# Second product of the last tile as seven block products, three of them after the last quartet

## The chip, the cores and the metric

The kernel runs on one core of a Trainium2 chip. The metric is the device time of one execution in microseconds (us). Each result is the median of several runs; the profile is of one execution.

## The reference

Nystrom attention for 4 batches, 8 heads, 576 positions and head dimension 64 feeds two feed-forward blocks of 2304 tokens, model width 512 and inner width 2048. All inputs are fp32. The change is in the second block:

```python
h = x @ w_in                                                  # 2304x512 @ 512x2048
g = np.where(h > 0.0, h, alpha * (np.exp(np.minimum(h, 0.0)) - 1.0))
return (g @ w_out).astype(np.float32)                         # 2304x2048 @ 2048x512
```

## The kernel before

Attention and block 1 come first and end some 430 us after the start; block 2 fills the rest. It works in NTT = 3 tiles of 768 tokens, each of two halves of T2 = 384 tokens, and each tile in NQ = 8 quartets. A quartet makes 256 of the 2048 inner columns: r and r + 8 of 16 column blocks of 128, for both halves, so four blocks (i, c) of 128x384.

A product of two fp32 matrices is made of three matmuls: each operand is split into a high part (a cast) and a low part (the value less the cast), and high x high, high x low and low x high are added up. `to_pair` (ScalarE for the cast, VectorE or GpSimd for the low part) does the splitting.

**First product** (`quartet`). It already is a product of seven blocks in Winograd's form of Strassen's method: seven products of 2x2 blocks instead of eight, with sums before and after. The sums of x lie on chip for a tile (`x_places`, `load_x`), those of w_in come from DRAM (`load_in2`). Each of seven steps p runs one block product, six matmuls of 384 columns, into one of two PSUM banks "h". VectorE adds the running sums to it, and `elu` makes a block of g: an add on VectorE out of PSUM, two activations on ScalarE, a combine on VectorE, then the pair. The pairs lie in a ring of eight places.

**Second product** (`second`, before the change everywhere). Per quartet: six groups of 128 tokens x two column blocks x three terms = 36 matmuls with a 128x128 piece of g as the loaded weight and 512 columns of w_out as the moving operand. They add up over the eight quartets in six PSUM banks (tags "bk" and "x"), are copied out in the last quartet (`ob`) and stored. The pairs of w_out come from DRAM (`wo2p`, written in the first tile) into a ring of NS = 4 places, two per quartet (`load_out2`).

**Order.** All matmuls of block 2 go through `bmm`, which chains each to the one before: PE's order is that of the program text. The loop at the end of the kernel runs `quartet` step by step and after each step some five or six matmuls of the second product, which lags by one quartet and one step (`behind`). What is left after the last quartet is run by `run(behind)`: 42 matmuls of 512 columns. On the other engines a planner orders the instructions by a priority (`wanted`) and its own estimate of times, and each engine then runs them strictly in that order. All DMAs are issued from SP in order; a DMA that waits for its place holds up those behind it.

`load_x(t + 1, pool)` prepares the sums of x of the next tile on GpSimd during the current one, so GpSimd works in the first two tiles of block 2 and is idle in the third. `scratch` takes its room from a ring of three. The places of an odd tile's x are free while an even tile is worked on, and in the last tile no next tile fills them.

The profile names nearly every instruction by one line, L110, the helper that records it. Tiles therefore tell what is what: h and x are PSUM banks (x also the sums of x), w the pairs of w_out, wi those of w_in, gf/gh/gl/ghl the blocks of g and their parts, y the sum inside `elu`, a and u the running sums, ob the output rows. PE is TensorE, DVE VectorE, ACT ScalarE, POOL GpSimd, SP the engine that issues the DMAs.

Of the kernel before, what the change touches and what calls it, by code (L numbers as in the profile page):

```python
# [10 lines left out]
F32 = mybir.dt.float32  # L11
F32R = mybir.dt.float32r
# [3 lines left out]
ALU = mybir.AluOpType  # L16
# [15 lines left out]
def nystrom_ffn_kernel(ctx: ExitStack, tc, q, k, v, w_in1, w_out1, w_in2, w_out2, out):  # L32
# [32 lines left out]
    B, G, _, _, S = q.shape  # L65
    D = 64
    H = 4 * G
    NDM, DM = w_in1.shape[2], w_in1.shape[2] * 128
# [3 lines left out]
    HALF = S // 2  # L72
# [6 lines left out]
    T2 = 384  # L79
    NS2 = T2 // 128  # L80
# [8 lines left out]
    NQ = NKT // 2  # L89
    NTT = NT // (2 * T2)  # L90
    LAG = 1
    T1 = 320
    YB, UB, SE = 2, 3, 1
    PRE, NLEAD, EI, EO = 2, 2, 3, 4
# [41 lines left out]
    ft = ctx.enter_context(tc.tile_pool(name="ft", bufs=2, reuse_waits="tile"))  # L136
    att = ExitStack()
# [13 lines left out]
    def wanted(s):  # L151
        tc.cur_priority = int(1000 * (s + 100))
# [33 lines left out]
    wo2d = dram.tile([NKT, 128, DM], F32, name="wo2d")  # L186
    wi2d = dram.tile([NQ, 2, 128, W], F32, name="wi2d")
    wi2p = dram.tile([NQ, 2, 2, 128, 7 * 128], F32, name="wi2p")
    wo2p = dram.tile([NKT, 2, 128, DM], F32, name="wo2p")

    banks, marks = {}, {}

# [108 lines left out]
    def to_pair(f, h, l, eng=vec):  # L301
        act.copy(out=h, in_=f)
        sub(l, f, h.bitcast(F32), eng)
# [4 lines left out]
    wo, wo2, wi, free = {}, {}, {}, {}  # L308
# [55 lines left out]
    PLACES = [f"wo{(kk - 2) % (NKT + 1)}" for kk in range(NKT + 1)]  # L364
    NS = 4

    late_out = []

    def load_out2(q):

        for i in range(2):
            kk = q % NQ + i * NQ
            t = wop.tile([128, 2, DM], F32, name="w2", tag=PLACES[(2 * q + i) % NS])
            hl = t.bitcast(F32R)
            if q < NQ:
                l = t[:, 1, :]
                sp.dma_start(out=l, in_=wo2d[kk])
                to_pair(l, hl[:, 0, :], hl[:, 1, :], pool)
                late_out.append((wo2p[kk].rearrange("x p n -> p x n"), t))
            else:  # L380
                sp.dma_start(out=t, in_=wo2p[kk].rearrange("x p n -> p x n"))
            wo2[q, i] = hl[:, 0, :], hl[:, 1, :]
# [407 lines left out]
    def span(b, hf):  # L790

        n = T1 if b == 0 else HALF
        return (0, n) if hf == 0 else (n, S - n)
# [57 lines left out]
    gt, acc = {}, {}  # L851
# [113 lines left out]
    def bmm(*a):  # L965

        inst = mm(*a)
        if chain[0] is not None:
            after(inst, chain[0])
        chain[0] = inst.ins  # L970

    def elu(key, src, add):

        n = made[0] % 8
        made[0] += 1
        if n < GB:
            h = gp.tile([128, T2], F32R, name="gh", tag="gh")
            l = gp.tile([128, T2], F32R, name="gl", tag="gl")
        else:
            t = nat.tile([128, G, W], F32R, name="ghl", tag=("nh2", "nl2", "nh3")[n - GB])  # L980
            h, l = t[:, 0, 0:T2], t[:, 1, 0:T2]
        gf = ft.tile([128, T2], F32, name="gf", tag="gf", bufs=2)
        c = stg.tile([128, W], F32, name="y", tag="y", bufs=YB)[:, 0:T2]
        vec.tensor_tensor(out=c, in0=src, in1=add, op=ALU.add)
        act.activation(out=gf, in_=c, func=AF.Relu, scale=-1.0)
        act.activation(out=gf, in_=gf, func=AF.Exp, scale=-1.0)
        vec.scalar_tensor_tensor(out=gf, in0=gf, scalar=-1.0, in1=c, op0=ALU.add, op1=ALU.max)
        to_pair(gf, h, l)
        gt[key] = h, l

    made = [0]

    def quartet(q):
# [24 lines left out]
        elu((q, 0, 0), block(1, 1), a1)  # L1018
        yield
        add(u3, block(3, 5), u2)  # L1020
        yield
        ps = block(4, 3)
        elu((q, 1, 1), ps, u3)
        add(u2, ps, u2)
        yield
        elu((q, 1, 0), block(2, 6), u3)
        yield
        elu((q, 0, 1), block(6, 2), u2)
        yield

    def second(q):

        for s in range(2 * NS2):
            if q % NQ == 0:
                acc[s] = (banks["x"] if s > 1 else banks["att"]).tile(
                    [128, 512], F32, name="x", tag="x" if s > 1 else "bk"
                )[:, 0:DM]
            sl = slice(s % NS2 * 128, s % NS2 * 128 + 128)
            for i in range(2):
                gh, gl = gt[q, i, s // NS2]  # L1040
                wh, wl = wo2[q, i]
                for j, (x, w) in enumerate(((gh, wh), (gh, wl), (gl, wh))):
                    bmm(acc[s], x[:, sl], w, q % NQ == 0 and i == j == 0, q % NQ == NQ - 1 and i == 1 and j == 2)
                    yield
            if q % NQ == NQ - 1:
                ob = nat.tile([128, G, HALF], F32R, name="ob", tag=("ath0", "ath1", "atl0")[s % 3])
                ob = ob.bitcast(F32).rearrange("p g t -> p (g t)")[:, 0:DM]
                (vec.tensor_copy if s % 2 else act.copy)(out=ob, in_=acc[s])
                r0 = q // NQ * 2 * T2 + s * 128
                sp.dma_start(out=out[r0:r0 + 128, :], in_=ob)  # L1050

    NA = B * SB

# [138 lines left out]
    for i in range(END, NA):  # L1192
        b, r = i // SB, i % SB
# [39 lines left out]

    def seconds():
        for q in range(NTT * NQ):
            yield from second(q)

    flush()
    wanted(NA - 6)
# [1 line left out]
    behind, tail, xs, n = seconds(), late(), x0, 0  # L1241
    for q in range(NTT * NQ):
        wanted(NA + 4 * q - 2)
        if q:
            load_in2(q + 1) if q + 1 < NTT * NQ else None
        if q % NQ == XPACE and q // NQ + 1 < NTT:
            xs = load_x(q // NQ + 1, pool)
        steps_ = quartet(q)
        for p in range(7):
            if p == 2:  # L1250
                load_out2(q)
            wanted(NA + 4 * q + 4 * p / 7 + 4)
            if conv and p % 2 == 0:
                conv.pop(0)()
            next(xs, None)
            wanted(NA + 4 * q + 4 * p / 7)
            next(steps_)
            for _ in range(2):
                next(tail, None)
            while n < (7 * q + p + 1 - 7 - LAG) * 12 * NS2 // 7:  # L1260
                next(behind)
                n += 1
        run(steps_)
# [37 lines left out]
```

## Time and profile before

| what | value |
|---|---|
| median of 3 runs | 825.69 us (821.93 to 826.5) |
| span of the profiled execution (the page gives no other time of it) | 824.7 us |
| PE busy | 788.3 us, 96% of the span |
| DVE, ACT, POOL busy | 62%, 54%, 41% |
| chain that ended last: PE, DVE, DMA, ACT | 75%, 12%, 5%, 3% |
| matmuls of 384 columns (first product of block 2) | 1008, 205.7 us |
| matmuls of 512 columns (second product of block 2) | 864 in three groups |
[...]

Busy times of matmuls overlap: one counts until its modelled end, while the next has started. How long a matmul takes of PE's time is read from the starts of two that follow each other.

### The profile page before, as it was taken

The page shows a single profiled execution, that of the slowest core. Times are in us where ns is not written, and L with a number is a line of the kernel's source. Part 1 is how long each engine was busy: PE and PEld are TensorE (multiplying, and loading weights), DVE is VectorE, ACT ScalarE, POOL GpSimd, SP SyncE. Part 2 cuts the span into 40 slices and gives each one's busy share as a digit, 9 for nine tenths or more (in the row PEclk, how much of TensorE's full clock was granted, in tenths as well). Part 3 has the DMA queues.
Part 4 walks back from the last instruction along what each step waited for, and adds up shares of the span by engine and source line. Part 5 has one row for each costly group of instructions (what it writes and reads, how often), then busy time and mean ns, then how long its engine had stood idle before and what let it go on. Part 6 is the DMA issues. An engine that isn't in the chain of part 4 may idle for free.

```text
span 824.7 us, 15400 instructions
## 1 busy us (share of the span) xinstructions
PE 788.3 (96%) x5644; PEld 689.3 (84%) x5644; DVE 508.2 (62%) x1026; ACT 446.1 (54%) x977; POOL 335.8 (41%) x348
## 2 busy tenths in 40 slices
PE   6699999999999999999997999999999999999998
PEld 3476777688997889889997999988989999999996
DVE  6898677457645754486347677656665455545543
ACT  3687554656656656574555556646454334434433
POOL 2566566557654665456438654620560000000000
PEclk9799999999999999999999999999999999999999
DMA  9966932685667445662442476777744655753632
GB/s 331 404 174 226 318 109 85 189 275 186 210 215 261 157 140 177 223 192 100 154 161 89 166 282 235 272 255 267 275 157 156 223 182 180 257 201 141 211 121 77
DMA packets 95563, 165.63 MB, mean 201 GB/s; under 512 B 7232, under 2 KB 51264, under 8 KB 95488
## 3 DMA queue, kind: packets, MB, share of 16 engines
q1 hardware_dynamic: 95488, 164.66, 58.6%
q8 instruction: 44, 0.72, 0.4%
q14 instruction: 31, 0.25, 0.1%
HBM read 119.54 MB, written 45.09 MB: 200 GB/s over the span
## 4 chain that ended last, share of the span: by engine, by line
PE 75%; DVE 12%; DMA 5%; ACT 3%; issue 2%; POOL 2%; SPq 0%; DVEq 0%; ACTq 0%; POOLq 0%
PE x L110 40%; PE h L110 29%; PE bk L110 6%; DVE u L110 1%; DVE h L110 1%; DMA u<-in_moe_w_in 1%; DVE y L110 1%; DVE nl L110 1%; DVE w1c L110 1%; POOL x L110 1%; DVE gf L110 1%; DVE lm L110 1%; DMA qt<-in_q 1%; DMA kt<-in_k 1%; DVE st L110 1%
## 5 line engine op out<-in xcount | busy, mean ns | idle before, releaser
L110 PE MATMUL h<-x,wi 128*128 128x384 f32 x1008 | 205.7, 339 | 1.1 <-DVE u L110 0.6
L110 PE MATMUL x<-gh,wo 128*128 128x288 f32 (+1 forms) x896 | 198.6, 297 | 0.8 <-ACT xs L110 0.4
L110 PEld LDWEIGHTS h<-x,wi 128*128 128x128 f32 x1008 | 182.1, 189 | 14.9 <-DVE u L110 1.0
L110 PEld LDWEIGHTS x<-gh,wo 128*128 128x128 f32 x896 | 149.1, 188 | 11.0 <-issue 7.2
L110 PE MATMUL x<-gl,wo 128*128 128x288 f32 (+1 forms) x448 | 130.6, 294 | 0.0
L110 ACT CAST gh<-gf 128x288 fp32r<-128x288 f32 (+2 forms) x172 | 78.7, 458 | 82.0 <-DVE gf L110 81.8
L110 POOL TENSOR_TENSOR gl<-gf,gh 128x288 fp32r<-128x288 f32 (+1 forms) x100 | 83.9, 841 | 85.3 <-ACT gh L110 75.0
L110 PE MATMUL x<-w,gh 128*128 128x512 f32 x360 | 116.5, 394 | 1.0 <-ACT gh L110 1.0
L110 ACT ACTIVATE gf<-y 128x384 f32<-128x384 f32 x96 | 50.4, 525 | 101.3 <-DVE y L110 101.2
L110 DVE SCALAR_TENSOR_TENSOR gf<-gf,y 128x384 f32<-128x384 f32 x96 | 65.2, 680 | 58.0 <-ACT gf L110 57.9
L110 PE MATMUL x<-w,ghl 128*128 128x512 f32 x324 | 89.1, 392 | 0.0
L110 ACT ACTIVATE gf<-h,half_b 128x288 f32<-128x288 f32 (+2 forms) x128 | 63.7, 500 | 44.2 <-PE h L110 40.8
L110 PE MATMUL h<-atl,nh 128*128 128x288 f32 (+2 forms) x256 | 81.6, 319 | 6.2 <-DVE gf L110 2.4
L110 PEld LDWEIGHTS x<-gl,wo 128*128 128x128 f32 x448 | 84.2, 188 | 1.1 <-issue 0.9
L110 DVE SCALAR_TENSOR_TENSOR gf<-gf,h 128x288 f32<-128x288 f32 (+1 forms) x112 | 49.5, 443 | 56.4 <-ACT gf L110 55.8
L110 PE MATMUL h<-ath,nl 128*128 128x288 f32 (+2 forms) x256 | 76.5, 299 | 0.0
L110 PE MATMUL h<-ath,nh 128*128 128x288 f32 (+2 forms) x256 | 76.3, 298 | 0.0
L110 PEld LDWEIGHTS x<-w,gh 128*128 128x128 f32 x360 | 67.4, 189 | 10.6 <-ACT gh L110 1.5
L110 PE MATMUL x<-w,gl 128*128 128x512 f32 x180 | 71.1, 395 | 3.5 <-DVE gl L110 3.5
L110 PEld LDWEIGHTS x<-w,ghl 128*128 128x128 f32 x324 | 60.2, 188 | 8.4
L110 PEld LDWEIGHTS h<-atl,nh 128*128 128x128 f32 x256 | 48.4, 189 | 19.2 <-issue 8.8
L110 DVE TENSOR_TENSOR gl<-gf,gh 128x384 fp32r<-128x384 f32 (+1 forms) x72 | 46.3, 643 | 21.9 <-ACT gh L110 17.4
(151 smaller groups left out, 1263.3 us busy)
## 6 DMA issues: line engine op xcount, KB each, us to landing
wi<-wi2p SPq DMA_DIRECT2D x64, 448.0 KB, 4.9
w<-wo2p SPq DMA_DIRECT2D x32, 512.0 KB, 6.1
wi2p<-wi SPq DMA_DIRECT2D x32, 448.0 KB, 2.9
u<-in_moe_w_in SPq DMA_DIRECT2D x25, 512.0 KB, 4.5
w1c<-w1d SPq DMA_DIRECT2D x48, 256.0 KB, 4.3
ub<-in_moe_w_out SPq DMA_DIRECT2D x16, 512.0 KB, 10.4
u<-in_moe_w_out SPq DMA_DIRECT2D x16, 512.0 KB, 5.2
wo2p<-w SPq DMA_DIRECT2D x16, 512.0 KB, 3.7
```

The costliest lines, as they stand in the source:

```text
L110: inst = getattr(self.eng, name)(*a, **kw)
```

## The change

In the last tile (t = 2, `WINO`) the second product too is made in Winograd's form. The 2x2 blocks of g are (half i, column block c) and those of w_out are (r or r + 8, left or right 256 columns). Of the seven products of a quartet four run at the place of the old ones (`wino2`), 36 matmuls of 256 columns: three use blocks of g as they are, one uses the sum S4 = f - s2, made in `quartet` after the last `elu` (a subtraction on VectorE and a pair). The other three use s1, s2 and s3, made by GpSimd in the quartet and kept on chip as fp32 in the free places of x, 24 of 128x384. `late2` runs these three after the last quartet: for each, over eight quartets, three token groups and three terms, 72 matmuls of 256 columns. It makes their pairs AHEAD = 5 places ahead, loads their weights (12 DMAs of 512 KB), copies the accumulators of the first four products out of PSUM and adds each late product to the rows where it belongs; the rows are stored in halves of 256 columns.

The sums of w_out (`sums_out2`) are made once, in the eight quartets of the middle tile: two loads, four subtractions and a pair on GpSimd and ScalarE, two stores into `to2p` per quartet. Their room is two of the three scratch places.

```diff
+    def sums_out2(q):
+        raw = scratch(2, DM)
+        for i in range(2):
+            sp.dma_start(out=raw[:, i], in_=wo2d[q + i * NQ])
+        t = scratch(4, HDM)
+        (b21, b22), (b11, b12) = ((raw[:, i, 0:HDM], raw[:, i, HDM:]) for i in range(2))
+        sub(t[:, 0], b12, b11, pool)
+        sub(t[:, 1], b22, t[:, 0], pool)
+        sub(t[:, 2], b22, b12, pool)
+        sub(t[:, 3], t[:, 1], b21, pool)
+        yield
+        h = raw.bitcast(F32R).rearrange("p a n -> p (a n)").rearrange("p (j n) -> p j n", j=4)
+        to_pair(t, h, t.bitcast(F32R), pool)
+        yield
+        o = q % 2 * HDM
+        for x, y in ((0, h.bitcast(F32)), (1, t)):
+            sp.dma_start(out=to2p[:, q // 2, x, :, o:o + HDM].rearrange("j p n -> p j n"), in_=y)
+        yield
...
+    def load_wino2(q):
+        r, o = q % NQ, q % 2 * HDM
+        b, a = w2_place(), w2_place()
+        sp.dma_start(out=b[:, :, 0:HDM], in_=wo2p[r + NQ, :, :, 0:HDM].rearrange("x p n -> p x n"))
+        sp.dma_start(out=b[:, :, HDM:], in_=to2p[3, r // 2, :, :, o:o + HDM].rearrange("x p n -> p x n"))
+        sp.dma_start(out=a, in_=wo2p[r].rearrange("x p n -> p x n"))
+        wo2[q] = a.bitcast(F32R), b.bitcast(F32R)
...
     def quartet(q):
...
-        elu((q, 1, 0), block(2, 6), u3)
+        f = elu((q, 1, 0), block(2, 6), u3, None, not wino)
+        if wino:
+            pool.tensor_tensor(out=s1, in0=f22, in1=f, op=ALU.add)
+            sub(s2, s1, f11, pool)
+            sub(s3, f11, f, pool)
         yield
-        elu((q, 0, 1), block(6, 2), u2)
+        f = elu((q, 0, 1), block(6, 2), u2)
+        if wino:
+            sub(f, f, s2)
+            gt[q, 4] = g_pair()
+            to_pair(f, *gt[q, 4])
...
+    def wino2(q):
...
+        for n, (x, w, c) in enumerate((((1, 1), b, lo), ((0, 0), b, hi), ((0, 1), a, lo), (4, a, hi))):
+            x = gt[(q, *x) if n < 3 else (q, x)]
+            for s in range(NS2):
...
+                o = accw[k][:, n // 2 * HDM:n // 2 * HDM + HDM]
+                for j, (g, y) in enumerate(terms(x, (w[:, 0, c], w[:, 1, c]))):
+                    bmm(o, g[:, tok(s)], y, first and n < 2 and j == 0, end and n > 1 and j == 2)
+                    yield
...
+    def late2(t):
...
+        for n in range(AHEAD):
+            pair(n)
+        p1, p4, v = (row(i) for i in range(3))
+        def drain(n, s, ps):
+            if n == 0:
+                vec.tensor_tensor(out=v[s], in0=ps, in1=v[s], op=ALU.add)
+                vec.tensor_tensor(out=p1[s], in0=ps, in1=p1[s], op=ALU.add)
+            elif n == 1:
+                vec.tensor_tensor(out=p1[s], in0=ps, in1=p1[s], op=ALU.add)
+                sub(p4[s], p1[s], p4[s], pool)
+                store(t, 0, 0, s, p4[s])
+            else:
+                vec.tensor_tensor(out=v[s], in0=ps, in1=v[s], op=ALU.add)
+                store(t, 1, 1, s, v[s])
+                vec.tensor_tensor(out=p1[s], in0=ps, in1=p1[s], op=ALU.add)
+                store(t, 0, 1, s, p1[s])
...
+        for n in range(NDEF):
...
+            for r in range(NQ):
+                m = n * NQ // 2 + r // 2
+                if r % 2 == 0:
+                    for x in (2, 3) if m == 0 else (m + 3,):
+                        if x < NDEF * NQ // 2:
+                            load_late2(t, x)
+                pair(n * NQ + r + AHEAD)
...
+                for s in range(NS2):
+                    for j, (g, y) in enumerate(terms(pairs[n * NQ + r], (w[:, 0, c], w[:, 1, c]))):
...
+                        bmm(ps[s], g[:, tok(s)], y, start, r == NQ - 1 and j == 2 and not n == s == 0)
+                        yield
+            for s in range(NS2):
+                drain(n, s, ps[s])
...
-            yield from second(q)
+            yield from (wino2 if q // NQ in WINO else second)(q)
+            if q % NQ == NQ - 1 and q // NQ in WINO:
+                yield from late2(q // NQ)
...
+        more = sums_out2(q % NQ) if q // NQ == WINO[0] - 1 else iter(())
         for p in range(7):
             if p == 2:
                 load_out2(q)
...
+            if p == 4 and q % NQ == NQ - 1 and q // NQ in WINO:
+                load_late2(q // NQ, 0)
+                load_late2(q // NQ, 1)
+            if p in (0, 3, 6):
+                next(more, None)
```

## Rows read from the trace of the kernel before

**Rows 1.** Busy us of each engine, granted clock, DMA share, GB/s, by stretch

```profile
760.00:800.00 40.00, 40.00 (x201) 36.23 (x200) 21.09 (x39) 17.51 (x35) 0.00 (x0) 1.00 0.45 157
```

**Rows 2.** The chain that ended last, from 780 us: start, us, what

```profile
796.68 1.38 PE x L110 x6
...
807.90 1.15 PE x L110 x5
809.05 1.05 PE h L110 x6
810.10 10.68 PE x L110 x47
```

**Rows 3.** Timeline from 820 us: start, us, engine, operation [idle before]

```profile
820.06 1.85 SPq L110 DMA_DIRECT2D out<-ob  x2
820.86 0.69 DVE L110 COPY ob<-x 128x512 f32<-128x512 f32 x1 [2.03 <-PE x L110]
```

**Rows 4.** Timeline from 796 us, around the last first-product block

```profile
809.94 0.40 PE L110 MATMUL x<-w,gh 128*128 128x512 f32 x1
...
810.14 0.56 DVE L110 TENSOR_TENSOR y<-h,u 128x384 f32<-128x384 f32 x1
...
812.44 0.52 ACT L110 CAST ghl<-gf 128x384 fp32r<-128x384 f32 x1 [0.62 <-DVE gf L110]
...
812.99 0.56 DVE L110 TENSOR_TENSOR ghl<-gf,ghl 128x384 fp32r<-128x384 f32 x1 [0.58 <-ACT ghl L110]
...
815.85 4.92 PE L110 MATMUL x<-w,ghl 128*128 128x512 f32 x21
```

**Rows 5.** Timeline of PE in block 1, first and last of twelve matmuls

```profile
162.27 0.28 PE L110 MATMUL x<-gh,wo 128*128 128x256 f32 x1
...
163.58 0.28 PE L110 MATMUL x<-gh,wo 128*128 128x256 f32 x1
```

**Rows 6.** Timeline of POOL in the middle tile of block 2

```profile
595.02 1.33 POOL L110 TENSOR_TENSOR x<-xf,x 128x384 fp32r<-128x384 f32 x1
...
598.71 1.02 POOL L110 TENSOR_TENSOR x<-xf,x 128x384 fp32r<-128x384 f32 x1
```

**Rows 7.** Timeline of DVE in the middle tile of block 2

```profile
587.02 1.33 DVE L110 SCALAR_TENSOR_TENSOR gf<-gf,y 128x384 f32<-128x384 f32 x1 [0.69 <-ACT gf L110]
...
600.07 0.55 DVE L110 TENSOR_TENSOR u<-h,u 128x384 f32<-128x384 f32 x1
```

**Rows 8.** Timeline from 445 us, first tile of block 2

```profile
451.03 0.28 DVE L110 TENSOR_TENSOR u<-u,wi 128x128 f32<-128x128 f32 x1
...
452.83 0.50 PE L110 MATMUL x<-w,gl 128*128 128x512 f32 x1 [3.52 <-DVE gl L110]
...
454.08 2.04 PE L110 MATMUL h<-x,wi 128*128 128x384 f32 x6
...
455.92 0.63 PE L110 MATMUL x<-w,gh 128*128 128x512 f32 x1
```

**Rows 9.** Timeline of PE in the middle tile of block 2

```profile
607.10 1.31 PE L110 MATMUL h<-x,wi 128*128 128x384 f32 x6 [0.51 <-DVE y L110]
```

**Rows 10.** Groups of POOL by shape: count, busy us, mean ns, idle before

```profile
L110 POOL TENSOR_TENSOR y<-y,u 128x512 uint32<-128x512 uint32 x32 | 42.3, 1322 | 21.3 <-ACT gf L110 10.4 <-ACT xs L110 6.1 <-DVE y L110 2.1
...
L110 POOL TENSOR_TENSOR gl<-gf,gh 128x256 fp32r<-128x256 f32 x16 | 11.9, 746 | 9.1 <-ACT gh L110 9.1
```

**Rows 11.** Busy us by stretch, start of the middle tile

```profile
560.60:576.00 15.40, 15.40 (x78) 13.94 (x77) 9.07 (x17) 8.60 (x19) 0.00 (x0) 1.00 0.72 265
```

**Rows 12.** DMA from 796 us: GB/s in 40 slices, issues with landing

```profile
GB/s 0 0 0 88 343 371 382 251 26 0 0 0 0 0 0 0 0 0 0 0 0 0 0 0 0 0 11 325 40 303 91 337 0 357 117 257 63 303 0 0
...
w<-wo2p SPq DMA_DIRECT2D x2, 512.0 KB, 4.0
```

**Rows 13.** Tile w from 680 us: ns least, median, most

```profile
L110 PEld LDWEIGHTS x<-w,gh x140: 187/188/191, 680.1 to 815.2; 128*128 128x128 f32 x140
```

**Rows 14.** Busy us by stretch, with the granted clock, first tile of block 2

```profile
454.20:457.60 3.40, 3.40 (x11) 3.06 (x10) 2.62 (x5) 1.67 (x4) 3.40 (x3) 0.50 0.34 135
```

More of the change, by code (lines that the diff above doesn't have):

```diff
@@ L91, in nystrom_ffn_kernel @@
     LAG = 1
+    WINO = (2,)
+    HDM = DM // 2
+    NDEF = 3
+    AHEAD = 5
     T1 = 320
@@ L189, in nystrom_ffn_kernel @@
     wo2p = dram.tile([NKT, 2, 128, DM], F32, name="wo2p")
+    to2p = dram.tile([4, NQ // 2, 2, 128, DM], F32, name="to2p")
     banks, marks = {}, {}
@@ L367, in nystrom_ffn_kernel, with w2_place, load_late2 @@
     late_out = []
+    def sums_out2(q):
[16 more added lines that the diff above has]
+        yield
+    place = [0]
+    def w2_place():
+        place[0] += 1
+        return wop.tile([128, 2, DM], F32, name="w2", tag=PLACES[(place[0] - 1) % NS])
+    def load_wino2(q):
[5 more added lines that the diff above has]
+        wo2[q] = a.bitcast(F32R), b.bitcast(F32R)
+    def load_late2(t, m):
+        j, r = (1, 2, 0)[m // (NQ // 2)], m % (NQ // 2)
+        w = w2_place()
+        sp.dma_start(out=w, in_=to2p[j, r].rearrange("x p n -> p x n"))
+        wo2[t, "late", m] = w.bitcast(F32R)
     def load_out2(q):
+        if q // NQ in WINO:
+            load_wino2(q)
+            return
         for i in range(2):
             kk = q % NQ + i * NQ
-            t = wop.tile([128, 2, DM], F32, name="w2", tag=PLACES[(2 * q + i) % NS])
+            t = w2_place()
             hl = t.bitcast(F32R)
@@ L970, in bmm, with g_pair @@
         chain[0] = inst.ins
-    def elu(key, src, add):
+    def g_pair():
         n = made[0] % 8
@@ L981, in elu @@
             h, l = t[:, 0, 0:T2], t[:, 1, 0:T2]
-        gf = ft.tile([128, T2], F32, name="gf", tag="gf", bufs=2)
+        return h, l
+    def elu(key, src, add, gf=None, split=True):
+        if gf is None:
+            gf = ft.tile([128, T2], F32, name="gf", tag="gf", bufs=2)
         c = stg.tile([128, W], F32, name="y", tag="y", bufs=YB)[:, 0:T2]
@@ L987, in elu, with sum_places @@
         vec.scalar_tensor_tensor(out=gf, in0=gf, scalar=-1.0, in1=c, op0=ALU.add, op1=ALU.max)
-        to_pair(gf, h, l)
-        gt[key] = h, l
+        if split:
+            gt[key] = g_pair()
+            to_pair(gf, *gt[key])
+        return gf
     made = [0]
+    sums_t, extra_t = {}, {}
+    def sum_places(t):
+        places = [y for x in x_places(t + 1) for y in x]
+        extra_t[t] = places[NDEF * NQ:]
+        for r in range(NQ):
+            for j in range(NDEF):
+                sums_t[t * NQ + r, j] = places[NDEF * r + j]
     def quartet(q):
@@ L1017, in quartet @@
         yield
-        elu((q, 0, 0), block(1, 1), a1)
+        wino = t in WINO
+        if wino:
+            if q % NQ == 0:
+                sum_places(t)
+            f22, f11 = extra_t[t][q % 2 * 2:q % 2 * 2 + 2]
+            s1, s2, s3 = (sums_t[q, j] for j in range(NDEF))
+        else:
+            f22 = f11 = None
+        elu((q, 0, 0), block(1, 1), a1, f22)
         yield
@@ L1022, in quartet @@
         ps = block(4, 3)
-        elu((q, 1, 1), ps, u3)
+        elu((q, 1, 1), ps, u3, f11)
         add(u2, ps, u2)
         yield
-        elu((q, 1, 0), block(2, 6), u3)
-        yield
-        elu((q, 0, 1), block(6, 2), u2)
+        f = elu((q, 1, 0), block(2, 6), u3, None, not wino)
[3 more added lines that the diff above has]
+            sub(s3, f11, f, pool)
+        yield
+        f = elu((q, 0, 1), block(6, 2), u2)
+        if wino:
+            sub(f, f, s2)
+            gt[q, 4] = g_pair()
+            to_pair(f, *gt[q, 4])
         yield
@@ L1050, in second, with terms, tok @@
                 sp.dma_start(out=out[r0:r0 + 128, :], in_=ob)
+    def terms(x, w):
+        (xh, xl), (wh, wl) = x, w
+        return (xh, wh), (xh, wl), (xl, wh)
+    def tok(s):
+        return slice(s * 128, s * 128 + 128)
+    def wino2(q):
+        t, first, end = q // NQ, q % NQ == 0, q % NQ == NQ - 1
+        a, b = wo2.pop(q)
+        lo, hi = slice(0, HDM), slice(HDM, DM)
+        for n, (x, w, c) in enumerate((((1, 1), b, lo), ((0, 0), b, hi), ((0, 1), a, lo), (4, a, hi))):
+            x = gt[(q, *x) if n < 3 else (q, x)]
+            for s in range(NS2):
+                k = s + n % 2 * NS2
+                if first and n < 2:
+                    accw[k] = (banks["x"] if k > 1 else banks["att"]).tile(
+                        [128, 512], F32, name="x", tag="x" if k > 1 else "bk"
+                    )
+                o = accw[k][:, n // 2 * HDM:n // 2 * HDM + HDM]
+                for j, (g, y) in enumerate(terms(x, (w[:, 0, c], w[:, 1, c]))):
+                    bmm(o, g[:, tok(s)], y, first and n < 2 and j == 0, end and n > 1 and j == 2)
+                    yield
@@ new lines, in nystrom_ffn_kernel, with store, pair, row @@
+    accw = {}
+    def store(t, c, d, s, y):
+        r0 = t * 2 * T2 + c * T2 + s * 128
+        sp.dma_start(out=out[r0:r0 + 128, d * HDM:d * HDM + HDM], in_=y)
+    def late2(t):
+        pairs = {}
+        def pair(n):
+            if n < NDEF * NQ:
+                pairs[n] = g_pair()
+                to_pair(sums_t[t * NQ + n % NQ, (1, 2, 0)[n // NQ]], *pairs[n])
+        def row(i):
+            x = scratch(NS2, HDM)
+            return [x[:, s] for s in range(NS2)]
+        for n in range(AHEAD):
[9 more added lines that the diff above has]
+                store(t, 0, 0, s, p4[s])
+            else:
+                vec.tensor_tensor(out=v[s], in0=ps, in1=v[s], op=ALU.add)
[3 more added lines that the diff above has]
+        for s in range(NS2):
+            act.copy(out=p1[s], in_=accw[s][:, 0:HDM])
+            ob = nat.tile([128, G, HALF], F32R, name="ob", tag=("ath0", "ath1", "atl0")[s])
+            ob = ob.bitcast(F32).rearrange("p g t -> p (g t)")[:, 0:HDM]
+            vec.tensor_tensor(out=ob, in0=accw[s][:, HDM:], in1=p1[s], op=ALU.add)
+            store(t, 1, 0, s, ob)
+        for s in range(NS2):
+            act.copy(out=p4[s], in_=accw[NS2 + s][:, 0:HDM])
+            vec.tensor_tensor(out=v[s], in0=accw[NS2 + s][:, HDM:], in1=p1[s], op=ALU.add)
+        def bank2(n, s):
+            if n == 0:
+                return banks["h"].tile([128, 512], F32, name="h", tag="h")
+            if n == 1 and s < 2:
+                return banks["att"].tile([128, 512], F32, name="x", tag="bk")
+            return banks["x"].tile([128, 512], F32, name="x", tag="x")
+        for n in range(NDEF):
+            wanted(NA + 4 * (t + 1) * NQ + 4 + 4 * n)
+            ps = [bank2(n, s) for s in range(NS2 - (n == 0))]
+            ps = [ps[0][:, 0:HDM], ps[0][:, HDM:], ps[1][:, 0:HDM]] if n == 0 else [p[:, 0:HDM] for p in ps]
+            for r in range(NQ):
+                m = n * NQ // 2 + r // 2
[4 more added lines that the diff above has]
+                pair(n * NQ + r + AHEAD)
+                w = wo2[t, "late", m]
+                c = slice(r % 2 * HDM, r % 2 * HDM + HDM)
+                for s in range(NS2):
+                    for j, (g, y) in enumerate(terms(pairs[n * NQ + r], (w[:, 0, c], w[:, 1, c]))):
+                        start = r == 0 and j == 0 and not (n == 0 and s == 1)
+                        bmm(ps[s], g[:, tok(s)], y, start, r == NQ - 1 and j == 2 and not n == s == 0)
+                        yield
+            for s in range(NS2):
+                drain(n, s, ps[s])
```

## Prediction

> **What bounds the kernel now.** First I read the busy time of the engines in stretches, because a mean over the span hides the stages. [...] Next the chain of waits: in one period PE runs six first-product matmuls of 384 columns (1.05 us) and five second-product matmuls of 512 columns (1.15 us), seven periods to a quartet (in one of them six, 1.38 us). After the last six it runs 47 of 512 columns alone [rows 2]; one copy and one store follow [rows 3]. The chain is PE from end to end; no other engine and no DMA stands in it here until 820.8 us.
>
> The page gives the profiled execution's span, 824.7 us, and no other time of it; the median of the runs is 825.69 us, so 1.0 us lies around the span. The sum is made against the span, and the difference is carried to the median.
>
> **The change, part by part.**
>
> *The matmuls.* Before, a quartet's second product is 36 matmuls of 512 columns; 8 quartets make 288. Of these 42 run after the last first-product block (the 47 of the chain less 5 of the quartet before). After, a quartet issues 4 products x 3 token groups x 3 terms = 36 matmuls of 256 columns, 288 in all, and 3 x 8 x 3 x 3 = 216 more of 256 columns run at the end. Price before: the seven x-pieces of a quartet last 6 x 1.145 + 1.38 = 8.25 us for 36, 229 ns each [rows 2]; in the tail 46 steps go from 809.94 to 820.38 us (the last one ends at 820.77 and lasts 0.39), 227 ns each [rows 4]. So 246 x 0.229 + 42 x 0.227 = 65.9 us. Price after: block 1 has twelve matmuls of 256 columns back to back, the first at 162.27 and the last at 163.58 us, 119 ns apart [rows 5]. All 504 at this price make 60.0 us. But 512 columns cost 2 ns more between first-product blocks than alone, so 246 of the narrow ones may cost 121.5 ns: 60.6 us. Gain 5.3 us; 5.9 at the clean price, 4.8 if the surcharge is twice as large.
>
> These twelve starts are 119 ns apart though each matmul has its own weight load, so the loads are hidden there. [...]
>
> *The seam.* PE's order is written out, so it can't fill a hole with later work. After the last first-product block (ended at 810.10) come 10 matmuls of quartet 22, then products (1,1), (0,0), (0,1) of quartet 23 with 9 each, then the product with the sum S4, whose operand is made last. At 119 ns PE reaches that one after 37 matmuls, at 809.94 + 4.40 = 814.34. The operand's chain is in the rows: add at 810.14, two activations, the combine, cast at 812.44, low part until 813.55 [rows 4]. Then come the new subtraction f - s2, a cast and a low part, 0.56 + 0.52 + 0.56 with gaps of 0.03: cast ready at 814.70, low part at 815.29. That alone makes PE wait 0.4 us, and 0.4 again before the third matmul: 0.8 us, the lower end. But s2 hangs on POOL: s1, then s2, after the combine of (1,0), which with the shorter period of about 1.67 us ends some 0.6 to 1.1 us after the block. A POOL operation of this size takes 1.02 us undisturbed and 1.33 beside DVE [rows 6], so s2 is there 2.7 to 3.8 us after the block, one operation later if s3 is taken before it. And beside POOL a DVE operation on two SBUF operands takes 1.33 us instead of 0.56 [rows 7]; two of them stand in this chain: 1.5 us more. Upper end 0.8 + 1.5 + 1.1 = 3.4 us. I take 1.9, a little below the middle, since s3 need not come first. Pairs for the late products are made on the same two engines meanwhile; 24 x 0.56 = 13 us of DVE and 24 x 0.52 = 12 us of ACT lie beside 25.7 us of late matmuls, so that stretch itself stays PE's.
>
> *The end.* Before, one copy of 0.69 us follows the last matmul, ends 0.78 us after it, and the last store is issued 0.36 later [rows 3]. After, the three groups of the last product end 0.36 us apart and need two adds each. No row has 128x256 from PSUM: 384 columns take 0.56 us [rows 4], 128 columns 0.28 [rows 8], so I put 0.42. Six of them from 0.68 us before PE's end last until 1.9 us after it: 1.1 us more, and 0.1 for stores that queue on SP at 0.36 each. I take 1.2. Bounds: at 0.28 the last group's two adds alone count, about 0.3 with the queue of stores; at 0.56 it is 1.9.
>
> *DVE inside the eight quartets.* A quartet shrinks from 15.6 to 7 x 1.055 + 36 x 0.121 = 11.7 us. DVE has 15 operations of 0.56 us in it before and 16 after: 8.9 us, 76%. A first-product bank must be read before the block two periods later starts: 1.25 us to the block's end and 0.56 for the read leave 1.5 of the new 3.35 us as slack, where there were 2.6. Three POOL sums per quartet, 3.1 to 4 us, hold a DVE operation up by 0.77 us each time. The slack mostly covers it; I charge 0.4 in all, bounds 0 and 4.1 (0.51 us, the one such PE wait in the last two tiles [rows 9], in each of eight quartets).
>
> [...]
>
> *The sums of w_out in the middle tile.* Per quartet: two loads of 256 KB, four POOL subtractions of 256 columns (0.75 each), one of 1024 (256 columns take 0.75 and 512 take 1.32 [rows 10]; by that slope 2.5), an ACT cast, two stores of 512 KB. That is 5.5 us of POOL, which is idle at 560 to 576 us, and 1.5 MB in 15.7 us, 96 GB/s on top of 265 there [rows 11]; PE stayed full under those 265, and slices with loads alone reached 382 [rows 12]. Hidden, but for the ACT cast: ACT runs in order, so the cast's wait for POOL holds back the activations behind it, and by them DVE and PE. That I charge with 0.3, bounds 0 and 4.1 (the 0.51 us of [rows 9] eight times).
>
> *Late weights.* Twelve loads of 512 KB, one per 2.14 us, each issued three tiles ahead (6.4 us). Landing took 4.0 us when two ran alone, at up to 382 GB/s [rows 12]. The tail needs 245 GB/s. I take 0.
>
> Sum: -5.3 + 1.9 + 1.2 + 0.4 + 0.3 = -1.5 us: span 823.2, time 824.2 us. A change of 0.5%, 4.1 us here, is about what a measurement of this kernel can tell from none.
>
> **Rivals.**
>
> *The seam is hidden.* [...] Chance, with what lies near it, 0.25.
>
> *The clock falls at the seam.* [...] Chance 0.12.
>
> *The lock reaches PE (slower).* One mechanism: POOL's sums hold a DVE operation, the bank read queued behind it comes later than the slack of 1.5 us (2.6 in the middle tile), PE stops 0.51 us. In each of 16 quartets that is 8.2 less the 0.7 charged: 6.0 above before, 831.7 us; from 13 of them on it decides. For it: the 1.33 us, and the wait of 0.51 came beside POOL. Against: it came once during 22 POOL operations. Chance 0.14.
>
> *Transfers bind.* If the tail gets 200 GB/s, its 6.3 MB last 31.5 us, not 25.7: 5.8 more, 830.0 us. Against it the 382 GB/s. Chance 0.04.
>
> *The loads of weights are not hidden* where narrow matmuls stand between wide blocks. Priced at the 188 ns that a load is busy [rows 13], a narrow one costs 69 ns more: 504 x 0.069 = 35 us, 859 us. Against it the 119 ns. Chance 0.02.
>
> **How the numbers follow.** Forecast 0.43, seam hidden 0.25, clock 0.12, lock 0.14, transfers 0.04, loads 0.02. Faster 0.25, within 0.5% 0.55, slower 0.20. The range goes from 819.5, two us beyond the hidden seam, to 830.0, short of the lock's full price; it leaves out about 2 in 10. The forecast's own range is 821.6 to 828.
>
> **What would show it.** Narrow matmuls 119 to 122 ns apart and a quartet of 11.7 us in the last tile; a PE wait on DVE or ACT of 1 to 3 us some 4 us after the last first-product block; late matmuls without a hole for 25.7 us; six adds at the end. The prediction is wrong if the quartet takes over 12.2 us, if PE waits on a DMA in the tail, or if PE has waits in the middle tile that it did not have.

## The result: 836.92 us, slower, and the profile after

The median is 836.92 us (834.99 to 839.56) against 826.22 us for the kernel before, run beside it: a ratio of 1.012, 95% interval [1.0089, 1.0151]. The forecast was 824.2 us, no change; the time lies 6.9 us above the range's upper end of 830.0.

Where it went can be read by cutting both profiles at the same four matmuls: the first first-product block of each tile of block 2, the last such block, and PE's modelled end. Each number is a difference of starts in the timeline of PE; the last seven kernels are told of below.

| us | until block 2 | first tile | middle tile | last tile, to the last block | last block to PE's end | rest | span |
|---|---|---|---|---|---|---|---|
| before | 431.3 | 127.9 | 126.7 | 123.0 | 11.9 | 3.9 | 824.7 |
| after | 429.9 | 128.4 | 135.0 | 96.2 | 40.1 | 4.9 | 834.6 |
| sums_only | 431.4 | 127.8 | 136.8 | 123.0 | 11.9 | 3.9 | 834.8 |
| sums_nostore | 429.4 | 128.0 | 130.4 | 123.0 | 11.9 | 3.9 | 826.5 |
| cover | 432.3 | 127.2 | 135.3 | 96.2 | 39.0 | 4.9 | 834.9 |
| cover_places | 430.5 | 126.8 | 135.4 | 96.2 | 34.0 | 4.9 | 827.8 |
| u2_own | 432.3 | 127.1 | 130.6 | 96.2 | 40.2 | 4.9 | 831.3 |
| repaired | 432.5 | 124.8 | 130.0 | 96.2 | 34.4 | 4.9 | 822.8 |
| before_u2_pair | 433.2 | 124.3 | 126.8 | 123.0 | 11.9 | 3.9 | 823.2 |

So the last tile did what the diff says, 26.8 us less before its last block, and two other places took it back and more: the middle tile 8.4 us, and the stretch after the last block, which grew by 28.2 us. Most of these are the matmuls moved there; some 6.6 us are not. (cover_places runs the same matmuls in this stretch in 34.0 us, 0.5 of it a wait; 40.1 less 33.5 is 6.6.)

The PE timeline of the changed kernel, rows from one period of the last tile (start, us, engine, operation):

```profile
787.92 1.22 PE L114 MATMUL h<-x,wi 128*128 128x384 f32 x6
788.97 0.28 PE L114 MATMUL x<-w,gl 128*128 128x256 f32 x1
789.09 0.40 PE L114 MATMUL x<-w,gh 128*128 128x256 f32 x2
...
789.57 1.22 PE L114 MATMUL h<-x,wi 128*128 128x384 f32 x6
```

A block and its five narrow matmuls take 789.57 - 787.92 = 1.65 us, and 0.60 us hold five matmuls: 120 ns each, like the 119 of block 1 [rows 5]. A quartet lasts 11.6 to 11.7 us, from the third of the tile on.

The middle tile, same view, the two rows with more than 0.2 us of idle time before them:

```profile
617.13 1.31 PE L114 MATMUL h<-x,wi 128*128 128x384 f32 x6 [1.93 <-DVE u L114]
...
637.20 2.29 PE L114 MATMUL h<-x,wi 128*128 128x384 f32 x6 [4.08 <-DVE u L114]
```

Before, the one such row in this tile was 0.51 us [rows 9]. The second wait is followed by six matmuls in 2.08 us, not 1.05: the clock had fallen (0.56 in the second row below). Busy time by stretch of the changed kernel (length, then PE, PEld, DVE, ACT, POOL busy, granted clock, DMA share, GB/s):

```profile
600.00:640.00 40.00, 33.99 (x161) 30.01 (x161) 22.35 (x33) 18.28 (x34) 29.40 (x27) 0.96 0.65 228
637.20:641.00 3.80, 3.80 (x11) 3.45 (x12) 1.58 (x3) 1.90 (x3) 2.56 (x3) 0.56 0.21 73
...
710.00:790.00 80.00, 80.00 (x534) 79.75 (x533) 62.73 (x111) 43.83 (x89) 24.13 (x21) 1.00 0.69 237
790.00:797.00 7.00, 5.11 (x36) 4.47 (x34) 6.74 (x10) 4.47 (x10) 3.56 (x3) 1.00 0.47 152
797.00:804.60 7.60, 5.75 (x25) 5.31 (x26) 5.52 (x13) 3.47 (x9) 0.00 (x0) 0.55 0.32 91
804.60:829.70 25.10, 25.09 (x210) 24.89 (x208) 12.87 (x29) 8.21 (x16) 2.65 (x3) 1.00 0.63 203
```

The seam shows the same pair of signs, PE idle for 1.9 us of 7 and then a mean granted clock of 0.55 over 7.6 us. After that PE is full until its end, at 1.00.

What the second wait of the middle tile hung on, from the timelines of DVE, POOL and SP:

```profile
629.99 0.55 DVE L114 TENSOR_TENSOR y<-h,a 128x384 f32<-128x384 f32 x1
...
636.58 0.56 DVE L114 TENSOR_TENSOR u<-h,a 128x384 f32<-128x384 f32 x1 [2.70 <-DMA to2p<-u]
```

```profile
629.84 2.49 POOL L114 TENSOR_TENSOR u<-u 128x1024 fp32r<-128x1024 f32 x1 [0.19 <-ACT u L114]
635.28 2.90 POOL L114 TENSOR_TENSOR u<-u 128x256 f32<-128x256 f32 x4 [2.94 <-DMA to2p<-u]
```

```profile
629.79 12.33 SPq L114 DMA_DIRECT2D to2p<-u  x4
```

The running sum (u<-h,a) stands on DVE behind a later step's add (y<-h,a): the planner had put it back. It needs a scratch place, and the three places now hold the sums too. It started at 636.58, after a wait put down to a store of the sums. GpSimd's next unit waited for the same stores until 635.28.

The first wait, 1.93 us, from the timelines of POOL and ACT:

```profile
604.76 2.72 POOL L114 TENSOR_TENSOR u<-u 128x1024 fp32r<-128x1024 f32 x1
613.64 1.43 POOL L114 TENSOR_TENSOR xf<-xf,x 128x384 f32<-128x384 f32 x1 [6.16 <-DMA xf<-x1d]
```

```profile
615.10 0.51 ACT L114 CAST x<-xf 128x384 fp32r<-128x384 f32 x1 [1.50 <-POOL xf L114]
615.52 0.51 ACT L114 CAST gh<-gf 128x384 fp32r<-128x384 f32 x1
```

The load of x for the next tile was issued at 606.77, behind the traffic of the sums, and landed 6.8 us later. GpSimd waited 6.16 us for it, ScalarE in its order 1.50 us for GpSimd, and the cast of g behind it came late for VectorE. This chain is read from the rows; no run changes that load alone.

The seam, from the timelines of PE, POOL, DVE and ACT:

```profile
796.37 0.50 PE L114 MATMUL x<-w,ghl 128*128 128x256 f32 x2 [1.62 <-ACT ghl L114]
797.57 1.86 PE L114 MATMUL x<-w,ghl 128*128 128x256 f32 x7 [0.70 <-DVE ghl L114]
800.71 2.51 PE L114 MATMUL x<-w,ghl 128*128 128x256 f32 x9 [1.28 <-ACT ghl L114]
```

```profile
793.06 2.29 POOL L114 TENSOR_TENSOR x<-x,gf 128x384 f32<-128x384 f32 x2 [8.70 <-DVE gf L114]
795.32 1.31 POOL L114 TENSOR_TENSOR x<-x,x 128x384 f32<-128x384 f32 x1
```

```profile
792.43 0.55 DVE L114 SCALAR_TENSOR_TENSOR gf<-gf,y 128x384 f32<-128x384 f32 x1
793.14 1.35 DVE L114 TENSOR_TENSOR gl<-x,gh 128x384 fp32r<-128x384 f32 x1 [0.16 <-ACT gh L114]
794.42 1.35 DVE L114 SCALAR_TENSOR_TENSOR gf<-gf,y 128x384 f32<-128x384 f32 x1
795.69 1.35 DVE L114 TENSOR_TENSOR ghl<-x,ghl 128x384 fp32r<-128x384 f32 x1
...
797.90 0.54 DVE L114 TENSOR_TENSOR gf<-gf,x 128x384 f32<-128x384 f32 x1
```

```profile
790.94 0.51 ACT L114 CAST gh<-x 128x384 fp32r<-128x384 f32 x1
791.36 0.51 ACT L114 CAST ghl<-x 128x384 fp32r<-128x384 f32 x1
...
795.80 0.51 ACT L114 CAST ghl<-gf 128x384 fp32r<-128x384 f32 x1 [1.58 <-DVE gf L114]
...
798.18 0.38 ACT L114 COPY u<-x 128x256 f32<-128x256 f32 x1 [1.46 <-PE x L114]
...
799.74 0.51 ACT L114 CAST ghl<-x 128x384 fp32r<-128x384 f32 x1
800.15 0.51 ACT L114 CAST ghl<-gf 128x384 fp32r<-128x384 f32 x1
```

The first two waits, 2.3 us, are those of product (0,1): its cast came at 795.80 and its low part at 796.97, after the combine of 794.42 to 795.77. Work for the late pairs was ahead of that chain: the two casts from 790.94 on ScalarE, and on VectorE a low part of 1.35 us from 793.14. Only the third wait, 1.3 us, is that of S4. GpSimd began when the combine of (1,0) ended (792.98), took s1 and s3 first and s2 last (795.32 to 796.63). Three VectorE operations beside it took 1.35 us each; low parts of this shape took 0.56 before, with GpSimd idle [rows 4]. And the cast of S4, free to run when f - s2 ended at 798.44, stood on ScalarE behind three copies of accumulators and a cast for a late pair, until 800.15.

### The profile page after: what moved, and what is told of

Read it like the earlier page. It is cut to its first block, busy times and chain, and to the rows that moved or that the text cites. A ratio compares the mean times of both kernels' runs of the same rounds, so it can differ in the third digit from the quotient of the medians.

```text
span 834.6 us, 16149 instructions
## 1 busy us (share of the span) xinstructions
PE 786.9 (94%) x5860; PEld 698.2 (84%) x5860; DVE 546.4 (65%) x1076; ACT 466.0 (56%) x1012; POOL 413.5 (50%) x415
## 4 chain that ended last, share of the span: by engine, by line
PE 63%; DMA 13%; DVE 9%; ACT 5%; POOL 4%; issue 3%; SPq 1%; DVEq 0%; POOLq 0%; ACTq 0%
PE x L114 33%; PE h L114 26%; PE bk L114 5%; DMA u<-in_moe_w_out 3%; DMA u<-in_moe_w_in 3%; DMA to2p<-u 2%; POOL u L114 2%; DVE u L114 2%; DVE gf L114 1%; ACT u L114 1%; SPq L114 1%; DMA qt<-in_q 1%; ACT gf L114 1%; DMA u<-wo2d 1%; DMA x<-x1d 1%
## 5 line engine op out<-in xcount | busy, mean ns | idle before, releaser
L114 PEld LDWEIGHTS h<-x,wi 128*128 128x128 f32 x1008 | 179.4, 190 | 17.8 <-DVE u L114 8.9
L114 PE MATMUL x<-gl,wo 128*128 128x288 f32 (+1 forms) x448 | 130.6, 294 | 0.0
L114 ACT CAST gh<-gf 128x288 fp32r<-128x288 f32 (+2 forms) x160 | 72.4, 453 | 88.1 <-DVE gf L114 87.7
L114 PE MATMUL x<-w,gh 128*128 128x512 f32 (+1 forms) x420 | 113.2, 347 | 1.3 <-ACT gh L114 1.3
L114 DVE SCALAR_TENSOR_TENSOR gf<-gf,y 128x384 f32<-128x384 f32 x80 | 67.9, 849 | 41.8 <-ACT gf L114 41.8
L114 PE MATMUL x<-w,ghl 128*128 128x512 f32 (+1 forms) x378 | 86.6, 355 | 3.9 <-ACT ghl L114 3.1
L114 ACT ACTIVATE gf<-h,half_b 128x288 f32<-128x288 f32 (+2 forms) x128 | 63.7, 499 | 42.8 <-PE h L114 40.1
L114 POOL TENSOR_TENSOR u<-u 128x256 f32<-128x256 f32 (+1 forms) x43 | 49.8, 1172 | 67.0 <-DMA u<-wo2d 31.9
L114 PEld LDWEIGHTS x<-w,gh 128*128 128x128 f32 x420 | 74.4, 190 | 7.7 <-ACT gh L114 1.8
L114 PE MATMUL x<-w,gl 128*128 128x512 f32 (+1 forms) x210 | 73.0, 348 | 3.8 <-DVE gl L114 3.8
L114 PEld LDWEIGHTS x<-w,ghl 128*128 128x128 f32 x378 | 64.1, 196 | 10.9 <-ACT ghl L114 4.0
L114 ACT ACTIVATE gf<-y 128x384 f32<-128x384 f32 x80 | 42.0, 525 | 48.6 <-DVE y L114 48.5
```

Source lines behind the costliest of these rows:

```text
L114: inst = getattr(self.eng, name)(*a, **kw)
```

## Experiments

Two theories of the middle tile: *places and queues* (the sums hold two of three scratch places until their stores have landed, and fill SP's queue) and *the port lock* (GpSimd's sums hold VectorE up: in the changed kernel a VectorE combine took 2.29 us at 605.61 beside one of them, and 0.55 at 609.01 with GpSimd idle; that a port or a lock does it no run shows). Two of the seam: *order* (PE must wait for the operand made last) and *a chain that is late wherever it is used*. Each ratio is to the kernel before, run beside it; where two runs were made beside different ones, their ratios compare better than their times.

**sums_only**: the kernel before plus the sums alone (`sums_out2` as in the change, called here).

```diff
+        more = sums_out2(q % NQ) if q // NQ == 1 else iter(())
...
+            if p in (0, 3, 6):
+                next(more, None)
```

> The kernel before, with only the sums of w_out in the middle tile added; nothing reads what they store. Places-and-queues theory (the sums hold two of three scratch places until their stores have landed, and the running sum u of the next quartet waits for one): the middle tile takes all of its loss, +7 to +9 us against before, with a PE wait on DVE u of about 4 us in that tile and another of about 2. Port-lock theory (GpSimd's sums hold VectorE up): also +7 to +9. Rival (the middle tile only suffers because later work of the last tile is planned into it): +0 to +2.

835.34 us, ratio 1.0121 [1.0086, 1.0156]: as slow as the whole change. The middle tile takes 10.1 us more, with waits of 1.93, 4.26 and 0.90 us. The sums suffice; the rival is out. Here the clock fell behind the wait of 1.93 us as well, which it had not in the changed kernel:

```profile
617.69 1.61 PE L111 MATMUL h<-x,wi 128*128 128x384 f32 x6 [1.93 <-DVE u L111]
```

```profile
618.50:621.90 3.40, 3.40 (x11) 2.94 (x11) 1.88 (x3) 1.12 (x3) 3.40 (x5) 0.50 0.16 54
```

**sums_nostore**: the same without the stores.

```diff
-        o = q % 2 * HDM
-        for x, y in ((0, h.bitcast(F32)), (1, t)):
-            sp.dma_start(out=to2p[:, q // 2, x, :, o:o + HDM].rearrange("j p n -> p j n"), in_=y)
-        yield
```

> As the one before, but the sums are not stored at all (the two stores per quartet are left out; loads, GpSimd and ScalarE work stay). Places-and-queues: the places come free some 5 us earlier and SP has no stores to hold, so no more than +2.5 us against before and no wait of 4 us. Port-lock: GpSimd does the same work, +7 to +8 stays.

828.24 us, ratio 1.0036 [1.001, 1.0063]. With all of GpSimd's work kept, the middle tile costs 3.7 us, not 10.1: GpSimd's hold on VectorE alone is not the loss. PE still waited 1.7, 0.8 and 0.3 us there. The 3.0 us by the ratio are a little above the 2.5 expected. This run takes away the stores' hold on the places and their place in SP's queue together; u2_own tells the two apart.

**u2_own**: the changed kernel with the running sum in a place of its own.

```diff
-                    xs = ft.tile([128, nt], F32, name="xs", tag="xs", bufs=NDM)
+                    xs = ft.tile([128, nt], F32, name="xs", tag="xs", bufs=3)
...
-        u2 = scratch(1, T2)[:, 0]
+        u2 = ft.tile([128, T2], F32, name="u2", tag="xs", bufs=3)
```

> The changed kernel, with the running sum u of a quartet in a place of its own (taken from the four places of the drain of block 1, which get three wider ones), so that the scratch places are the sums' alone. Places theory: the wait of 4 us on DVE u in the middle tile and the half clock behind it go, 5 to 6 us less than the changed kernel; the wait of about 2 us in the quartet before stays, because it hangs on a late load. Queue theory (the stores hold up SP's queue and the DMA engines, and the place is only named by chance): at most 1.5 us less. The drain with three places may cost block 1 up to 1 us.

830.99 us, ratio 1.0059 [1.0037, 1.0081], 5.9 less than the changed kernel (5.0 by the ratios). The stores are all there, the wait of 4 us is not: it was the place. The running sum is again ahead of the later add, in the DVE timeline:

```profile
631.29 0.55 DVE L114 TENSOR_TENSOR u<-h,a 128x384 f32<-128x384 f32 x1
631.75 0.54 DVE L114 TENSOR_TENSOR y<-h,a 128x384 f32<-128x384 f32 x1
```

The middle tile falls from 135.0 to 130.6 us, so the place accounts for 4.4 of its 8.4. The other 4.0 stay; the waits left in the tile come to 3.0. The expectation erred in one point: the wait of 1.9 us went too, and one of 1.6 us came, behind a VectorE combine.

**before_u2_own**: the price of that edit on the kernel before.

> The kernel before with the same move of u and of the drain's places: the price of that edit by itself. Within 1 us of before by every theory; if block 1's drain needs its fourth place, up to 3 us slower.

829.95 us, ratio 1.0027 [0.9998, 1.0056]. Inconclusive by its interval; in the profile block 2 starts at 436.5 us, 5.1 later than before, which points at the drain with three places.

**cover**: the last quartet's products (0,1) and S4 run among the first late product's matmuls.

```diff
-    AHEAD = 5
+    AHEAD = 3
...
+        if end and len(todo) == 4:
+            todo = (0, 1)
...
+                if n == 0 and r in (1, 3):
+                    yield from wino2(t * NQ + NQ - 1, (2 + r // 2,))
+                    front(r // 2)
```

> The changed kernel, with the last quartet's products (0,1) and S4 moved in among the matmuls of the first late product (after its second and fourth quartet), their accumulators copied out there, and pairs made 3 places ahead, not 5. Seam theory (PE's order forces it to wait for the operand made last, and the clock then falls): the waits of 1.6, 0.7 and 1.3 us and the half clock go, 5 to 6.5 us less than the changed kernel. Rival (the operand chain is so late that the wait only moves): 0 to 1.5 us less. The middle tile is untouched.

837.4 us, ratio 1.014 [1.0108, 1.0173]: no gain, both theories missed. The operand waits of over 0.2 us fell from 3.6 to 0.5 us, but the PE timeline shows a new wait in their place, with a granted clock of 0.59 afterwards (last row):

```profile
804.30 1.24 PE L114 MATMUL h<-w,ghl 128*128 128x256 f32 x9
808.88 0.35 PE L114 MATMUL h<-w,ghl 128*128 128x256 f32 x1 [3.34 <-DMA w<-to2p]
```

```profile
808.88:813.00 4.12, 4.12 (x22) 4.12 (x23) 1.43 (x4) 0.74 (x2) 0.00 (x0) 0.59 0.08 31
```

The fourth late weight goes into the place that the moved products read, so its load starts later than before.

**cover_places**: the third and fourth late weight in places of the first product's weights, free by then.

```diff
+        if m in (2, 3):
+            w = nat.tile([128, G, W], F32, name="w2", tag=("nh0", "nl0")[m - 2])
+        else:
+            w = w2_place()
```

> The run with the two last products moved (cover), with the third and fourth late weight loaded into the places of the first product's weights, which are free after the last block, and not into the place that the moved products still read. Seam theory: neither the operand waits nor the DMA wait of 3.3 us is left, 5 to 6.5 us less than the changed kernel. Rival (the tail is bound by the transfers of late weights): a DMA wait of 2 us or more stays elsewhere, at most 3 us less.

830.97 us, ratio 1.0064 [1.0034, 1.0093], 6 less than the changed kernel (4.6 by the ratios). From the last block to PE's end 34.0 us, not 40.1; one operand wait of 0.5 us is left. Order, with the transfers' places, was the seam.

**pre**: s2 with one GpSimd operation after f.

```diff
+        if wino:
+            sub(s2, f22, f11, pool)
...
-            pool.tensor_tensor(out=s1, in0=f22, in1=f, op=ALU.add)
-            sub(s2, s1, f11, pool)
+            pool.tensor_tensor(out=s2, in0=s2, in1=f, op=ALU.add)
+            pool.tensor_tensor(out=s1, in0=f22, in1=f, op=ALU.add)
```

> The changed kernel, with s2 made as (f22 - f11) + f: the difference ahead of the last two blocks, so that one GpSimd operation instead of two or three lies between f and s2, at the price of one GpSimd operation more per quartet. If GpSimd's chain sets the seam: 1 to 2.5 us less than the changed kernel. If the casts and copies queued ahead on ScalarE and the port lock set it: within 0.7 us, or slower by the extra operation.

837.59 us, ratio 1.0159 [1.0114, 1.0204]: not faster. PE's waits at the seam sum to 2.8 us against 3.6, and from the last block to PE's end it takes 39.6 us against 40.1. Of GpSimd's part in the seam no more than this shows; the queue of ScalarE was not tested by itself.

**u2_own_cover**: both repairs.

> Both repairs in one kernel. If the two causes are separate they add up: 10 to 12 us less than the changed kernel, 825 to 827 us, level with before; what is then left of the expected gain of 5 us is the late load in the middle tile with its half clock (3 us) and the longer end (1 us).

827.92 us, ratio 1.0015 [0.9998, 1.0032]. The two savings by ratio, 0.61% and 0.56%, would leave 1.0003; the interval holds that, so they add up as far as it tells. The time lies 0.9 us above what was expected.

**repaired**: cover_places, with the drain of block 1 in two places of two rows each, so that u takes one without costing block 1.

```diff
-                    xs = ft.tile([128, nt], F32, name="xs", tag="xs", bufs=NDM)
+                    if dm % 2 == 0:
+                        xs2 = ft.tile([128, 2, HALF], F32, name="xs", tag="xs", bufs=2)
+                    xs = xs2[:, dm % 2, 0:nt]
...
-        u2 = scratch(1, T2)[:, 0]
+        u2 = ft.tile([128, 2, HALF], F32, name="u2", tag="xs", bufs=2).rearrange("p a n -> p (a n)")[:, 0:T2]
```

> Both repairs, with the drain of block 1 in two places of two rows each (as much room as its four of one), of which u takes one in block 2. If the price of the first form of u's own place was the drain's missing fourth place: 2 to 3 us less than with both repairs before, 824.5 to 826 us, level with before or up to 1.5 us faster. If it was the planner's different order elsewhere: no gain, 827 to 828 us.

822.68 us, ratio 0.9957 [0.9938, 0.9977]: faster than both kernels, and beyond what was expected. The table shows where the surplus lies: the first tile, which the change doesn't touch, is 3 us shorter. That part is luck.

**before_u2_pair**: the kernel before with that place for u, and nothing of the change.

> The kernel before with u in its own place as in the repaired kernel, and nothing of the change: does the repaired kernel owe its 4 us to the seven products or to that place? In the repaired profile the wait for a low part in the first tile of block 2 is 1.6 us, not 3.5, and no half clock follows. If that comes from the place of u alone, this kernel is 2 to 4 us faster than before, 823 to 825 us, and the seven products, repaired, are worth 0 to 2 us. If it comes from the change, this kernel is within 1 us of before.

824.06 us, ratio 0.9972 [0.9951, 0.9994]. That edit alone gives about two thirds of the gain (0.28 of 0.43%). PE's wait for a low part in the first tile, 3.52 us [rows 8], is here, in the PE timeline:

```profile
452.70 0.50 PE L110 MATMUL x<-w,gl 128*128 128x512 f32 x1 [1.59 <-DVE gl L110]
```

It is not u's own place that does this: in u2_own and before_u2_own u has one too, and the wait is 3.59 and 3.58 us. The form of the drain's places has put VectorE's work in the first tile in another order. The low part that PE waits for, in the kernel before (first fence) and here (second), from the timelines of DVE:

```profile
451.23 0.28 DVE L110 TENSOR_TENSOR u<-wi,u 128x128 f32<-128x128 f32 x1
451.43 1.34 DVE L110 TENSOR_TENSOR gl<-gf,gh 128x384 fp32r<-128x384 f32 x1
```

```profile
452.10 0.55 DVE L110 TENSOR_TENSOR gl<-gf,gh 128x384 fp32r<-128x384 f32 x1
452.57 1.09 DVE L110 TENSOR_TENSOR u<-u,wi 128x128 f32<-128x128 f32 x1
```

Block 2 starts 1.9 us later here, and the low part still ends 0.1 us sooner. Why the planner chose so is not shown.

The table tells the rest against this kernel: the repaired one is 3.3 us shorter from the last tile on (135.5 against 138.8) and 3.2 us longer in the middle tile. So the repaired products are worth the difference of two ratios, 0.15% or 1.2 us, which these intervals don't tell from nothing.

**split**: the 1024-column subtraction in four pieces. In the repaired kernel this VectorE combine (first fence) met that GpSimd operation (second):

```profile
637.72 2.64 DVE L114 SCALAR_TENSOR_TENSOR gf<-gf,y 128x384 f32<-128x384 f32 x1 [2.04 <-ACT gf L114]
```

```profile
637.52 2.42 POOL L114 TENSOR_TENSOR u<-u 128x1024 fp32r<-128x1024 f32 x1
```

```diff
-        to_pair(t, h, t.bitcast(F32R), pool)
+        act.copy(out=h, in_=t)
+        for j in range(4):
+            sub(t.bitcast(F32R)[:, j], t[:, j], h.bitcast(F32)[:, j], pool)
```

> The repaired kernel, with the 1024-column GpSimd subtraction of each unit of sums made as four of 256 columns. Lock theory (a VectorE operation on two SBUF operands waits for the whole GpSimd operation): the PE wait of 1.6 us in the middle tile, behind a VectorE combine of 2.6 us, goes, 1 to 3 us less than the repaired kernel (with half clock). Rival (GpSimd is simply full there): within 0.7 us.

823.89 us, ratio 0.9966 [0.9947, 0.9985]: no gain over the repaired kernel. The wait of 1.6 us is gone, others of 1.1 and 0.5 us have come; the middle tile takes 129.3 us, not 130.0. In the repaired kernel the combine took 2.64 us and ended 0.4 us after the GpSimd operation; here the same combine took 0.97 us (638.50 in the DVE timeline).

**split_pre**: both.

> As split, with s2 = (f22 - f11) + f. With the seam covered by late matmuls the chain of s2 has time, so nothing is expected: within 1 us of split. A gain of over 1 us would show that GpSimd's chain still sets a wait.

822.48 us, ratio 0.9952 [0.9932, 0.9972]: as expected, no difference from split or repaired that the intervals show.

## Why the prediction was wrong, step by step

- *The matmuls*, -5.3 us: right. The last tile is 26.8 us shorter, and with the seam covered the rest is 22.1 us longer (34.0 against 11.9), 0.5 of it a wait: -4.7 to -5.2. The 119 ns of block 1 held (120 in the last tile), so the loads stayed hidden, and the rival of loads that show is out. (After the last block PE has 11 matmuls of quartet 22 left, not 10, before and after; that moves the seam by 0.12 us.)
- *The sums of w_out in the middle tile*, "0.3, bounds 0 and 4.1": this step failed. The tile grew by 8.4 us: PE's waits by 5.9 (6.4 against 0.5), and the lower clock behind the second wait (0.51 from 637.20 to 640.60 us) cost some 1.7 more, an estimate: half of these 3.4 us. GpSimd's time and the bytes were counted, but not the places: that a unit holds two of three scratch places from its load until its stores land, and that u draws on the same ring. The ring of three and the two places were known; who else uses the ring was not asked. u2_own shows that the place accounts for 4.4 us. The other 4.0 are more than the term too, and are explained only in part: by waits behind GpSimd's sums and, as far as the rows go, the late load. The prediction's own sign of being wrong, waits in the middle tile that weren't there before, is what came.
- *The seam*, 1.9 us, bounds 0.8 and 3.4: this failed too. The waits came to 3.6 us, above the upper end. s2 was last, as the upper end had it. But the chain was worked out from rows of a kernel that makes no late pairs, and the pairs for the late products were charged to the stretch behind it. They stood ahead of the chain: the combine of (1,0) ended 2.4 us after the last block (790.62), not 0.6 to 1.1, and 2.3 of the 3.6 us came at product (0,1), whose operand had been taken as ready. ScalarE's copies ahead of S4's cast were not in it either. The lower clock behind the waits added about 2.8 us, an estimate: half of the 5.55 us that PE was busy from 797.5 to 804.4 us, at a granted 0.51. The rival "the clock falls at the seam" was given 0.12, though the first tile before shows such a fall: 0.50 over 3.4 us behind a wait of 3.52 us [rows 8, 14].
- *The end*, 1.2 us: right, 1.0. Six adds in 2.08 us, the last at 831.09, 1.4 us after PE; the last store was issued at 832.24:

```profile
829.01 2.08 DVE L114 TENSOR_TENSOR u<-x,u 128x256 f32<-128x256 f32 x6 [6.04 <-PE x L114]
829.46 2.78 SPq L114 DMA_DIRECT2D out<-u  x6
```

- *DVE inside the eight quartets*, 0.4: measured 0. No PE row of the last tile before its last block has idle time; DVE was busy 62.7 of 80 us, 78%.
- *Late weights*, 0: right as the change orders them. The reserve was thin, as cover showed.
- *The lock reaches PE*, the rival of the slower side, gave 831.7 us by 16 small stops. The sign was its, the mechanism was not: two long stops, one from a place, the other, by the rows, from a late load. What it calls a lock is, in the rows, a VectorE operation on two SBUF operands that takes 1.33 us beside GpSimd (587.02 [rows 7], GpSimd busy from 586.92 to 587.94) and 0.56 with GpSimd idle [rows 4]; how the two engines hold each other up no run shows. The 0.55 us of the operation at 600.07 [rows 7] was not measured beside GpSimd: it starts behind GpSimd's operation, which ended at 599.73 [rows 6]. One out of PSUM that did run beside GpSimd, in the kernel before, took 0.54 us (first fence; GpSimd in the second):

```profile
588.27 0.54 DVE L110 TENSOR_TENSOR y<-h,u 128x384 f32<-128x384 f32 x1
```

```profile
588.01 2.51 POOL L110 TENSOR_TENSOR xf<-x,xf 128x384 f32<-128x384 f32 x2
```

In all the span grew by 9.9 us where -1.5 was forecast: 8.4 in the middle tile, 2.4 from the last tile to the end (-26.8, 28.2 and 1.0), -0.9 ahead of them.

Not settled: the 3.4 us that the repaired kernel's middle tile still costs, of which waits explain 2.7; why one wait of 1.93 us was followed by the lower clock and another was not; and why kernels in which block 1 is unchanged reach block 2 between 429.4 and 432.3 us.

## What to carry to other kernels

When a change adds a side stream to a full stage, count the buffers that it holds, from its load until its store has landed, and who draws on the same ring, before its engine time. A saving of 5 us in matmuls was lost here by one wait of 4 us, with the 1.7 us that by estimate the lower clock cost behind it. Work out the chain of an operand with everything that the change itself puts on the same engines. And run the kernel before with the repairs that don't belong to the change: here one of them gave two thirds of the gain. Order the matmuls so that an operand made last has other work ahead of it, and check that moving them doesn't keep a weight's place longer.

## What the runs showed of the hardware that was not expected

- After a PE wait of 4.08 us the granted clock was 0.51 over 3.4 us (0.56 over 3.8 us). At the seam it fell after waits of 1.6 and 0.7 us (0.55 over 7.6 us, with a third wait of 1.3 us in them). A single wait of 1.93 us was followed by 0.50 over 3.4 us in sums_only and by no fall in the changed kernel (1.00 from 617.13 to 623 us).
- A VectorE combine of 0.56 us took 2.64 beside a GpSimd subtraction of 1024 columns (repaired), and 1.35 beside GpSimd operations of 384 (changed kernel).
